# First pass of an induced-attention and two-FFN kernel: a smaller first group, two groups' x in both layouts from memory, the inducing points from another queue

## The chip, the cores and the metric

One NeuronCore of a Trainium2 chip runs the whole kernel. The metric is device time in microseconds (us) of one execution; lower is better. Engines are named as the profile names them: PE (TensorE matmul), PEld (TensorE weight load), DVE (VectorE), ACT (ScalarE), POOL (GpSimd), SP (SyncE, which here only issues DMAs; a small q behind an engine's name is its instruction queue).

## What is computed

With x of 12480 tokens x 128 and 32 inducing points of 128, all f32:

```python
def mab(q, kv):
    s = scale * (q @ kv.T); a = softmax(s)
    return a @ kv
h = mab(I, x)            # the first pass: 32 queries over all tokens
y = mab(x, h)            # every token over 32 keys
g = y @ w_in;  y = (g * clip(g + 3, 0, 6) / 6) @ w_out       # d_ff 2048
g = y @ w_in2; out = relu(g) ** 2 @ w_out2
```

Nothing after the first pass can begin before h is whole, since its softmax runs over all tokens. The four weight matrices are stored as 64-bit words that the kernel itself turns into f32, in pieces of 512 words a partition: a0 to a3 (w_in), b0 to b3 (w_out), c and d (the second FFN).

## The kernel before, in words

The span has two parts. The **first pass** (about 37 us) computes h; the rest (about 920 us) is a software pipeline over 25 chunks of up to 512 tokens. The change touches the first pass alone.

The first pass runs over eight groups g0 to g7 (`GROUPS`; each entry is a block of rows, and a block holds 4 x 128 tokens, or 4 x 48): g0 has 1024 tokens, g1 to g4 2048 each, g5 1216 (it is kept in the tile `xlast` for later), g6 and g7 1024 each. `xT` and `x` are the same tokens in two layouts in memory. For one group:

- `load_group` brings x transposed (tile `xg`, three buffers, L298; the group g5 goes to `xlast`), and makes the tile `xn` (three buffers, made in the order of the groups) for x in its natural layout.
- `scores`: 8 matmuls (L340, tile `s1`), then DVE takes the maximum (L344, into `kept`).
- x in its natural layout: `turn_x` transposes each block on PE (4 transposes, L360) and ACT copies it out (L365). For the groups in `NATURAL` (g7 alone) nothing is turned; `load_natural` reads it from memory instead (L303).
- `exps` on ACT (L350), `turn_e`: transposes of the exponentials on PE (L373) and a DVE copy (L375, L378); `accumulate`: 8 matmuls a block (L385) and an ACT copy (L389).

The order is software-pipelined by hand and kept: each engine does its instructions in the order in which the code has them. In iteration g: loads of x up to g+3, `scores(g)`, `turn_e(g-1)`, `turn_x(g)`, `exps(g)`, a tick, `accumulate(g-1)`, a tick. Ticks are numbered from 0, two an iteration, and `EARLY` says what of the weights is converted at each: tick 10 does a2's third and a3's second stage, tick 11 (the last thing of g5's iteration) a3's third stage and b0's first, tick 12 b0's second, tick 13 its third, tick 16 (after the loop's last accumulation) b1's first. A piece's first stage is an ACT multiplication of the raw words (L180) and two DVE instructions on them (L188, L192), so ACT and DVE both wait there for the piece's load; the second stage is two more on DVE (L201, L209), the third an addition on POOL (L221).

All loads are issued by SP in one fixed order, `LOADS`; `load_until` only says when the code issues them. A load whose buffer is still in use waits on SP, and everything behind it in the list waits too. At the end of the pass h is scaled and written (L447 to L464); the short chain up to the first matmuls of the pipeline (`fill` are matmuls into nothing, L261) follows.

```python
    for g in range(NG):
        load_until(("x", min(g + 3, NG - 1)))
        load_until(("n", g))
        scores(g)
        if g:
            turn_e(g - 1)
```

Of the kernel before, what the change touches and what calls it, by code (L numbers as in the profile page):

```python
# [26 lines left out]
LINE = 256  # L27


GROUPS = [(128,) * 2] + [(128,) * 4] * 4 + [(128, 128, 48), (128,) * 2, (128,) * 2]  # L30
KEPT = 5
TURN_V = {}
NATURAL = {7}


LOADS = [("x", 0), ("x", 1), ("x", 2), ("a", 0), ("x", 3), ("a", 1), ("x", 4), ("a", 2), ("a", 3),
         ("x", 5), ("b", 0), ("x", 6), ("x", 7), ("b", 1), ("n", 7), ("b", 2), ("b", 3)]

# [31 lines left out]
def induced_attention_then_two_ffn(  # L72
# [11 lines left out]
    nc = tc.nc  # L84
# [9 lines left out]
    SCALE = 1.0 / math.sqrt(D)  # L94
    NG = len(GROUPS)
    run = [sum(blocks) for blocks in GROUPS]
    assert sum(run) * J == NT and D == P and J == 4
# [185 lines left out]
    with ExitStack() as pro:  # L283
# [5 lines left out]

        row = pp.tile([P, J, M], F32, name="row")  # L290
        sel, ind, inds = (row[:, i, :] for i in range(3))
        nc.sync.dma_start(ind, indT)
        xn = {}

        def load_group(g):
            n = run[g] * J
            xg[g] = xlast if g == KEPT else pp.tile([P, n], F32, tag="xg", name="xg", bufs=3)
            nc.sync.dma_start(xg[g], xT[:, t0[g]:t0[g] + n])  # L298
            xn[g] = pp.tile([P, len(GROUPS[g]) * J, D], F32, tag="xn", name="xn", bufs=3)

# [54 lines left out]
        def turn_x(g, b):  # L355
            blk, o = GROUPS[g][b], sum(GROUPS[g][:b])
            t = pps.tile([blk, J, D], F32, tag="xt", name="xt", bufs=4)
            for j in range(J):
                i = j * run[g] + o
                nc.tensor.transpose(t[:, j, :], xg[g][:, i:i + blk], ident)  # L360
            dst = xn[g][:blk].rearrange("p (j b) d -> p b j d", j=J)[:, b]
            if b in TURN_V:
                nc.vector.tensor_copy(dst, t)
            else:
                nc.scalar.copy(dst, t)  # L365

        def turn_e(g):
            nb = len(GROUPS[g])
            t = pps.tile([P, nb, P], F32, tag="xt", name="ett", bufs=4)
            et[g] = pp.tile([P, nb, P], F32, tag="et", name="et", bufs=2)  # L370
            for b, blk in enumerate(GROUPS[g]):
                o = sum(GROUPS[g][:b])
                nc.tensor.transpose(t[:blk, b, :], es[g][:, o:o + blk], ident)  # L373
            whole_blocks = sum(blk == P for blk in GROUPS[g])
            nc.vector.tensor_copy(et[g][:, :whole_blocks], t[:, :whole_blocks])  # L375
            for b in range(whole_blocks, nb):
                blk = GROUPS[g][b]
                nc.vector.tensor_copy(et[g][:blk, b], t[:blk, b])  # L378
# [42 lines left out]
        for g in range(NG):  # L421
# [8 lines left out]
            for b in range(len(GROUPS[g])):  # L430
                if g not in NATURAL:
                    turn_x(g, b)
# [453 lines left out]
```

## Time and profile before

| | |
|---|---|
| median of 3 runs | 958.47 us (958.36 to 959.15) |
| the profiled execution: its time / its span | 959.55 us / 957.8 us |
| mean granted TensorE clock | 0.998 |
| busy share: PE, PEld, DVE, ACT, POOL | 99%, 80%, 83%, 85%, 26% |
| moved by DMA | 34.28 MB, of it 14.88 MB in the first 60 us |

Rows of a timeline read: start in us, duration in us, engine, line, operation, output<-input, how many were merged, and in brackets how long the engine had been idle and what ended that. Start times count from the span's start. A matmul's row overlaps the next one's, since matmuls are pipelined. "Landing" of a load is the time from its issue to its completion.

### The profile page before, as it was taken

Reading aid. Unit: us, or ns where it says so; the run is one execution under the profiler, and the core shown is the slowest. Engines: PE = TensorE matmul, PEld = TensorE weight load, DVE = VectorE, ACT = ScalarE, POOL = GpSimd, SP = SyncE. Lnnn points to the kernel's source line nnn. Section 1 sums busy time; section 2 is a strip of 40 time slices with the busy share of each in tenths; the row PEclk is TensorE's granted clock in tenths of the full one; section 3 lists DMA queues with packets and bytes.
Section 4 is the critical chain, followed back from the end, with each engine's and each line's share of the span. In section 5 each row is a group of like instructions: output and inputs, shape, how many; then the busy total and the mean of one; then the engine's idle time right before and its main releaser. Section 6 shows DMA issues by size and latency. Waiting matters only on the chain.

```text
span 957.8 us, 12885 instructions
## 1 busy us (share of the span) xinstructions
PE 947.5 (99%) x4609; PEld 767.7 (80%) x4609; DVE 795.1 (83%) x971; ACT 813.0 (85%) x927; POOL 248.4 (26%) x412
## 2 busy tenths in 40 slices
PE   9799999999999999999999999999999999999998
PEld 7546678888888888888888888888888888888898
DVE  5887788888888888888888888888888888888774
ACT  6668888888888888888888888888888888889887
POOL 1233222222222222222222222222222222222222
PEclk9999999999999999999999999999999999999999
DMA  9621000000100000100000100010000100000000
GB/s 363 233 69 55 5 19 23 1 22 26 42 23 12 11 23 11 56 23 9 15 23 8 48 23 7 17 55 4 19 23 3 46 23 2 22 20 2 17 12 16
DMA packets 30671, 34.28 MB, mean 36 GB/s; under 512 B 7440, under 2 KB 24080, under 8 KB 30096
## 3 DMA queue, kind: packets, MB, share of 16 engines
q1 hardware_dynamic: 30608, 33.47, 10.5%
q8 instruction: 36, 0.59, 0.3%
q14 instruction: 27, 0.22, 0.1%
HBM read 21.18 MB, written 6.39 MB: 29 GB/s over the span
## 4 chain that ended last, share of the span: by engine, by line
PE 97%; DVE 2%; issue 0%; ACT 0%; POOL 0%; DVEq 0%; POOLq 0%
PE h L726 28%; PE oacc L697 27%; PE yacc L697 25%; PE h L649 9%; PE yacc L685 3%; PE oacc L685 1%; PE xt L360 1%; PE ps L513 1%; PE s L340 1%; PE hacc L385 0%; PE fill L261 0%; DVE cve L192 0%; DVE et L375 0%; DVE cve L188 0%; DVE m L495 0%
## 5 line engine op out<-in xcount | busy, mean ns | idle before, releaser
L658 DVE SCALAR_TENSOR_TENSOR g<-g,h 128x1024 f32<-128x1024 f32 (+2 forms) x200 | 238.8, 1194 | 119.5 <-ACT g L657 116.8
L657 ACT ACTIVATE g<-h,small 128x1024 f32<-128x1024 f32 (+2 forms) x200 | 219.1, 1096 | 115.5 <-PE h L649 111.6
L761 DVE TENSOR_TENSOR lo<-g,hi 128x1024 fp32r<-128x1024 f32 (+3 forms) x193 | 228.9, 1187 | 7.8 <-PE oacc L697 4.1
L677 DVE TENSOR_TENSOR lo<-g,hi 128x1024 fp32r<-128x1024 f32 (+2 forms) x184 | 219.1, 1191 | 0.8 <-POOL hi L669 0.8
L741 ACT ACTIVATE g<-g 128x1024 f32<-128x1024 f32 (+3 forms) x201 | 206.0, 1025 | 0.2
L737 ACT ACTIVATE g<-h 128x1024 f32<-128x1024 f32 (+3 forms) x201 | 199.3, 992 | 3.3 <-PE h L726 2.1
L753 ACT CAST hi<-g 128x1024 fp32r<-128x1024 f32 (+1 forms) x186 | 191.6, 1031 | 0.0
L669 POOL TENSOR_SCALAR hi<-g 128x1024 fp32r<-128x1024 f32 (+2 forms) x182 | 187.2, 1029 | 0.0
L726 PE MATMUL h<-yh,wl 128*128 128x512 f32 (+2 forms) x400 | 153.7, 384 | 0.0
L726 PE MATMUL h<-yh,wh 128*128 128x512 f32 (+2 forms) x400 | 153.7, 384 | 0.0
L726 PE MATMUL h<-yl,wh 128*128 128x512 f32 (+2 forms) x400 | 153.7, 384 | 0.0
L649 PE MATMUL h<-at,m 128*128 128x512 f32 (+2 forms) x400 | 129.3, 405 | 2.3 <-DVE m L495 2.0
L697 PE MATMUL oacc<-hi,wh 128*128 128x512 f32 (+2 forms) x384 | 116.5, 384 | 0.0
L697 PE MATMUL oacc<-hi,wl 128*128 128x512 f32 (+2 forms) x384 | 116.4, 384 | 0.0
L697 PE MATMUL oacc<-lo,wh 128*128 128x512 f32 (+2 forms) x384 | 116.4, 384 | 0.0
L796 POOL COPY small<-lo 128x1 f32<-128x1 f32 x115 | 21.8, 189 | 344.8 <-DVE lo L677 344.8
L697 PE MATMUL yacc<-hi,wl 128*128 128x512 f32 (+2 forms) x368 | 111.2, 383 | 0.0
L697 PE MATMUL yacc<-hi,wh 128*128 128x512 f32 (+2 forms) x368 | 111.2, 383 | 0.0
L697 PE MATMUL yacc<-lo,wh 128*128 128x512 f32 (+2 forms) x368 | 111.2, 383 | 0.0
L649 PEld LDWEIGHTS h<-at,m 128*128 128x128 f32 x400 | 74.4, 188 | 26.5 <-issue 8.7
L726 PEld LDWEIGHTS h<-yl,wh 128*128 128x128 f32 x400 | 75.1, 188 | 14.6
L726 PEld LDWEIGHTS h<-yh,wh 128*128 128x128 f32 x400 | 75.1, 188 | 14.2
(121 smaller groups left out, 920.5 us busy)
## 6 DMA issues: line engine op xcount, KB each, us to landing
outT<-osb SPq DMA_DIRECT2D x23, 256.0 KB, 2.2
xc<-in_xT SPq DMA_DIRECT2D x9, 512.0 KB, 4.6
xg<-in_xT SPq DMA_DIRECT2D x4, 1024.0 KB, 7.1
at<-ah SPq DMA_DIRECT2D x168, 16.0 KB, 1.8
at<-al SPq DMA_DIRECT2D x168, 16.0 KB, 1.8
raw<-in_w1a SPq DMA_DIRECT2D x4, 512.0 KB, 8.8
raw<-in_w1b SPq DMA_DIRECT2D x4, 512.0 KB, 7.5
raw<-in_w2a SPq DMA_DIRECT2D x4, 512.0 KB, 8.3
```

What stands on the lines that cost most here:

```text
L649: nc.tensor.matmul(h1[k][:, u, :size[c]], lhsT=m4[:, f * P:(f + 1) * P], rhs=a_t[c], start=True, stop=True)
L657: nc.scalar.activation(g1[k], h, AF.Relu, bias=three)
L658: nc.vector.scalar_tensor_tensor(out=g1[k], in0=g1[k], scalar=6.0, in1=h, op0=ALU.min, op1=ALU.mult)
L669: nc.gpsimd.tensor_scalar(out=hi1[k], in0=g1[k], scalar1=1.0, scalar2=1.0, op0=ALU.mult, op1=ALU.mult)
L677: nc.vector.tensor_tensor(out=lo1[k], in0=g1.pop(k), in1=hi1[k], op=ALU.subtract)
L685: nc.tensor.matmul(acc, lhsT=w[:, f * P:(f + 1) * P], rhs=g[:, u, :], start=(p == 0 and u == 0), stop=(p == NP - 1 and u == 1),)
L697: nc.tensor.matmul(acc, lhsT=w[:, f * P:(f + 1) * P], rhs=g[:, u, :], start=(p == 0 and n == 0), stop=(p == NP - 1 and n == 5),)
L726: nc.tensor.matmul(h2[k][:, u, :size[c]], lhsT=w, rhs=y, start=(n == 0), stop=(n == 2))
L737: nc.scalar.activation(g2[k][:, u, :], h[:, u, :n], AF.Relu)
L741: nc.scalar.activation(g2[k][:, u, :], g2[k][:, u, :], AF.Square)
L753: nc.scalar.copy(hi2[k][:, u, :], g2[k][:, u, :])
L761: nc.vector.tensor_tensor(out=lo2[k][:, u, :], in0=g[:, u, :], in1=hi2[k][:, u, :], op=ALU.subtract)
```

## The change

The first group has one block (512 tokens) instead of two; g6 has three blocks (1536 tokens) instead of two. So all groups together still hold 12480 tokens. g6 is added to the groups whose natural x is read from memory, so its `turn_x` goes and a load `("n", 6)` of 768 KB comes. The list of loads has that load between those of x for g6 and g7, and b0's load moves from ahead of g6's x to behind g7's. The load of the inducing points is issued by ACT instead of SP. `EARLY` is not changed.

```diff
-GROUPS = [(128,) * 2] + [(128,) * 4] * 4 + [(128, 128, 48), (128,) * 2, (128,) * 2]
+GROUPS = [(128,)] + [(128,) * 4] * 4 + [(128, 128, 48), (128,) * 3, (128,) * 2]
-NATURAL = {7}
+NATURAL = {6, 7}
 LOADS = [("x", 0), ("x", 1), ("x", 2), ("a", 0), ("x", 3), ("a", 1), ("x", 4), ("a", 2), ("a", 3),
-         ("x", 5), ("b", 0), ("x", 6), ("x", 7), ("b", 1), ("n", 7), ("b", 2), ("b", 3)]
+         ("x", 5), ("x", 6), ("n", 6), ("x", 7), ("b", 0), ("n", 7), ("b", 1), ("b", 2), ("b", 3)]
...
-        nc.sync.dma_start(ind, indT)
+        nc.scalar.dma_start(ind, indT)
```

## Rows read from the trace of the kernel before

**Rows 1.** Busy time of the page: us (share), instructions of each engine.
```profile
PE 947.5 (99%) x4609; PEld 767.7 (80%) x4609; DVE 795.1 (83%) x971; ACT 813.0 (85%) x927; POOL 248.4 (26%) x412
```
**Rows 2.** Timeline of PE and PEld in the first pass.
```profile
1.36 4.10 PE L261 MATMUL fill<-ident 128*128 128x128 f32 x18 [1.36 <-POOL ident masks.py:199]
5.39 1.08 PE L340 MATMUL s<-xg,row 128*32 128x256 f32 x8
6.41 1.14 PE L360 MATMUL xt<-ident,xg 128*128 128x128 f32 x8
...
7.47 0.16 PEld L340 LDWEIGHTS s<-xg,row 128*32 128x32 f32 x8 [0.17 <-DMA xg<-in_xT]
...
22.75 1.08 PE L385 MATMUL hacc<-xn,et 128*32 128x128 f32 x32
...
27.07 0.61 PE L340 MATMUL s<-xg,row 128*32 128x256 f32 x8
...
29.75 1.00 PE L385 MATMUL hacc<-xn,et 128*32 128x128 f32 x24 [0.71 <-DVE et L375]
```
**Rows 3.** Busy time by stretch: each engine's us (instructions), granted clock, DMA share, GB/s.
```profile
20.00:25.00 5.00, 5.00 (x75) 3.92 (x68) 4.30 (x9) 4.25 (x12) 1.29 (x2) 1.00 1.04 403
26.00:27.00 1.00, 1.00 (x35) 0.83 (x36) 0.97 (x2) 1.00 (x5) 0.26 (x1) 1.00 0.28 96
```
**Rows 4.** Timeline of SP's queue: when loads are issued.
```profile
0.74 0.39 SPq L292 DMA_DIRECT2D row<-in_indT  x1
...
1.18 0.42 SPq L298 DMA_DIRECT2D xg<-in_xT  x1
...
12.70 0.47 SPq L152 DMA_DIRECT2D raw<-in_w1b  x1
...
19.03 0.43 SPq L152 DMA_DIRECT2D raw<-in_w1b  x1
...
27.35 0.38 SPq L303 DMA_DIRECT2D xn<-in_x  x1
...
28.42 0.50 SPq L152 DMA_DIRECT2D raw<-in_w1b  x1
```
**Rows 5.** DMA issues, those five loads in that order: KB, us to landing.
```profile
xg<-in_xT SPq DMA_DIRECT2D x1, 512.0 KB, 3.7
...
raw<-in_w1b SPq DMA_DIRECT2D x1, 512.0 KB, 11.4
...
raw<-in_w1b SPq DMA_DIRECT2D x1, 512.0 KB, 8.9
...
xn<-in_x SPq DMA_DIRECT2D x1, 512.0 KB, 3.9
...
raw<-in_w1b SPq DMA_DIRECT2D x1, 512.0 KB, 6.1
```
**Rows 6.** Waits of SP's queue, 0 to 62 us: us in total, times, longest.
```profile
SPq L303 <- PE hacc L385: 7.8, 1, 7.8
```
**Rows 7.** DVE timeline around tick 11, and L192's durations (ns, min/median/max).
```profile
27.18 0.42 DVE L188 TENSOR_SCALAR cve<-raw 128x512 uint32<-128x512 uint32 x1
...
29.29 0.41 DVE L375 COPY et<-ett 128x256 f32<-128x256 f32 x1
...
L192 DVE TENSOR_SCALAR cve<-cve x7: 426/428/1393, 13.8 to 42.7; 128x512 f32<-128x512 f32 x7
```
**Rows 8.** Timeline of POOL at that time.
```profile
27.41 1.33 POOL L221 TENSOR_TENSOR wa<-cve,cva 128x512 int32<-128x512 int32 x1 [1.16 <-DVE cve L209]
```
**Rows 9.** PE after an idle stretch in the pipeline's first microseconds, timeline.
```profile
46.33 0.73 PE L649 MATMUL h<-at,m 128*128 128x512 f32 x2 [1.96 <-DVE m L495]
...
48.01 3.32 PE L685 MATMUL yacc<-g,w 128*128 128x512 f32 x4
...
52.19 1.88 PE L685 MATMUL yacc<-g,w 128*128 128x512 f32 x4
```
**Rows 10.** The same stretch by half microseconds: PE busy, granted clock, DMA share, GB/s.
```profile
47.50:48.00 0.50, 0.50 (x1) 0.50 0.68 240
```

## The prediction

> **What bounds the kernel now.** The busy times come first: PE is busy for 99% of the span [rows 1], so the pipeline after the first pass has no room, and whatever moves the end of the pass moves the end of the kernel by as much. The change touches the pass alone, so the rest is read there. PE's timeline shows it at work from 1.36 us, first on 18 matmuls into nothing and then on one group after another [rows 2]. It is the pace-maker up to the scores of g6 at 27.07; then it stands for 0.71 us, and `accumulate(5)` at 29.75 is let go by DVE's copy L375. So the last part of the pass hangs on DVE, and DVE's order around tick 11 says why: b0's first stage (L188 at 27.18, then L192) stands ahead of the maximum of g6 and of that copy [rows 7]. The third view is the stretches: the DMA engines are at a share of 1.04 with 403 GB/s from 20 to 25 us, and idle soon after, 0.28 at 26 to 27 us [rows 3]. A load is thus late or early by the bytes ahead of it.
>
> **The start.** Moving the inducing points off SP lets the first x be issued at 0.74 instead of 1.18 us, 0.44 earlier [rows 4]; ACT has nothing to do so early. That x was issued at 1.18 and landed 3.7 later, at 4.9 [rows 4, 5], while the fill matmuls still ran to about 5.4 [rows 2], so the first scores start no earlier than 0.3 us before, whatever the load does. What the smaller group gives lies in the PE work: scores and turning of g0 took 5.39 to 6.41 and 6.41 to 7.47, each halves, so 1.04 us goes. The scores of g1 waited 0.17 us for their x at 7.47 [rows 2]; that load now comes 0.44 + 0.64 us sooner (0.64 for 256 KB less ahead of it, worked out below), which just covers it. `accumulate(0)` and `turn_e(0)` lose a block too: 1.08/4 = 0.27 us [rows 2] and a little. I take 1.35 us for all of it, between 0.3 (only the start moves) and 1.6. The loads behind move 1.08, so up to 0.27 of the 1.35 may be waited away again.
>
> **g6's turning removed.** 12 transposes and their copies on ACT go. They are costed at nothing: PE stood idle for 0.71 us right behind them, waiting for DVE [rows 2]. DVE is not relieved. The block that left g0 is now in g6, at the end of the pass where nothing hides it: 0.27 us of `accumulate(6)` and up to 0.2 us (half of the 0.41 us that two blocks' copy takes [rows 7]) of each of DVE's copy and maximum. Between 0.3 and 0.7; I take 0.5 us lost.
>
> **The load of b0, the term that decides.** b0 was issued at 12.70 and landed 11.4 later, at 24.1; DVE wanted it at 27.18, so 3.1 us were spare. b1 was issued at 19.03 and landed 8.9 later, at 27.9. Between the two landings the queue brought 3 x 512 KB in 3.83 us, 1.28 us for 512 KB [rows 4, 5, 7]. After the change b0 stands behind g6's x (768 KB), g6's natural x (768 KB) and g7's x (512 KB), less 256 KB of g0: 1792 KB more, 4.48 us, and 0.44 earlier from the start: 28.1 us at best. But tick 11 is not moved, and the pass runs 1.35 us ahead, so ACT and DVE stop for b0 at about 25.8. The maximum of g6, the copy for `accumulate(5)` and everything of g6 and g7 stand behind it.
>
> It gets later if g6's natural x waits. SP's queue shows how its fellow did: g7's natural x waited 7.8 us on `accumulate` [rows 6] and went out at 27.35 [rows 4], just after `accumulate(4)`, though g2's buffer had long been free: buffers go round in the order in which the tiles are made, and g7's is g4's. By that g6's is g3's, free after `accumulate(3)`, which ended at about 23.65 (22.75 and its length [rows 2]), so now 22.3. g7's x and b0 queue on SP behind that wait. From the issue, g7's natural x took 3.9 us to 31.25, and b3, issued at 28.42, landed 6.1 later at 34.5, 1024 KB behind it [rows 4, 5]. So g6's lands at 22.3 + 3.9 + 0.64 = 26.8, and b0, also 1024 KB behind, between 26.8 + 2.56 = 29.4 and 26.8 + 3.27 = 30.1. I take 29.8, nearer to the late row, since that is the one which had a natural x at the head of the queue.
>
> From L188's start to `accumulate(5)` it was 29.75 - 27.18 = 2.57 us. In this L192 took 1.39 where its median is 0.43 [rows 7], beside POOL's addition at 27.41 [rows 8]; that addition (a3's third stage) will be over before b0 lands. 2.57 - 0.97 = 1.60 us is left. So `accumulate(5)` starts at 29.8 + 1.60 = 31.4, 1.65 us later than before (1.25 to 1.95). All that the start won is gone: DVE's clock for the rest is the landing of b0.
>
> **PE's clock.** PE has no turning to do meanwhile. With the pass 1.35 ahead, scores and `turn_e` end at about 27, and it stands until 31.4, over 4 us. Later in the trace it stood for 1.96 us before 46.33; from 47.5 on the granted clock is 0.50, that is 1.2 GHz, and four matmuls took 3.32 us where the next four took 1.88 [rows 9, 10]. The gap of 0.71 us is followed by no such thing. So 0 to 2.9 us (twice that loss) may be added; I take 1.7, that row's 1.44 and a little for the short matmuls behind, since the new gap is longer than the one that lost the clock.
>
> **Sum.** 1.65 + 0.5 + 1.7 = 3.85 us, of which the start's gain is already part. The profiled execution took 959.55 us (span 957.8); with 3.85 it is 963.4. It lies 1.1 above the median of the runs, 958.47, to which I add the same: 962.3 us. This case by itself reaches from 958.5 + 1.25 + 0.5 = 960.2 to 958.5 + 1.95 + 0.5 + 2.9 = 963.8.
>
> **Rivals.** *g6's natural x does not wait.* If the buffers are handed out by who is ready, g0's or g1's is free when SP comes to it, and b0 lands at 28.1. Then `accumulate(5)` starts at 29.7 as before, 0.5 is lost for the block and 0 to 1.7 for the clock (PE stands 2.7 us): 959.0 to 960.6 us. For it: nothing in the code forbids it. Against it: the 7.8 us that g7's waited.
>
> *b0 is in time, not slower.* The decision is at b0's landing: at 27.65 or before, 1.60 later `accumulate(5)` is 0.5 us sooner than before, which pays for the block; at 25.8 or before DVE doesn't wait at all, and the gain is 1.35 - 0.5 = 0.85, 957.6 us. It takes a b0 that overtakes the 1280 KB of natural x and g7's x ahead of it. The landings of before come in the order of issue, b0 24.1 and b1 27.9 with two loads between, which speaks against it. The Trainium skill, in DMA: Bandwidth & Descriptors, "Queues, rings and completion order", says that completion is not in order per issuing engine, as data transfers carry no barrier between them. By that rule b0 could land ahead of what was issued before it and this case would hold; no row here shows a load doing so.
>
> A further chance on this side: if the stretch at 1.2 GHz from 47.5 us does not come back in the shifted timing, 1.44 us are won in any case [rows 9].
>
> **How the numbers follow.** A difference of 0.2%, 1.9 us (956.55 to 960.4), is about what a measurement of this kernel can tell from none. The forecast gets 0.58, the first rival 0.20, the second 0.17; 0.05 is left for what I don't see. Slower by over 0.2%: 0.52 of the forecast, 0.04 of the first rival, 0.02 of the rest, 0.58. Faster by over 0.2% needs the second rival with the clock's 1.44 us as well: 0.08 with part of the rest. The same: 0.34. The range of 8 in 10 goes from 957.0, a little under the second rival's own time, to 964.5, a little beyond the forecast's upper end for a clock that stays low longer; the forecast's own range is 960.2 to 963.8.
>
> **What the profile would show.** Right: b0's load issued at about 23 and landing at 29 to 30; ACT's L180 and DVE's L188 idle for some 4 us before tick 11, ended by a DMA on `raw`; `accumulate(5)` at 31 to 32; PE idle from 27, with matmuls of twice the length behind it. The scores of g1 at 6.1 to 6.5 and of g2 over a microsecond earlier than before. The first rival: g6's natural x issued at about 14, right behind g6's x. The second: b0's L188 at 26 with no wait. The prediction is wrong if DVE does not wait for b0, or if the pass's end, the write of h, comes less than 1 us later than before.

## The result, and the profile after

The changed kernel takes 966.16 us (median of 8 executions, 961.31 to 966.53) against 958.93 us for the kernel before (8 on the same chip, 958.36 to 959.9): a ratio of 1.0061, 95% interval 1.0046 to 1.0077. It is slower, as forecast, but by 7.2 us, where 3.85 had been summed up and 964.5 was the upper end of the range. The profiled execution took 966.22 us with a span of 964.4, which is 6.6 above the span profiled before.

PE's timeline in the changed kernel answers to [rows 2] and, in its last row, to [rows 9]:

```profile
5.40 0.62 PE L340 MATMUL s<-xg,row 128*32 128x128 f32 x8
5.94 0.66 PE L360 MATMUL xt<-ident,xg 128*128 128x128 f32 x4
6.53 1.07 PE L340 MATMUL s<-xg,row 128*32 128x512 f32 x8
...
25.91 0.83 PE L340 MATMUL s<-xg,row 128*32 128x384 f32 x8
26.67 0.55 PE L373 MATMUL ett<-ident,es 128*128 128x128 f32 x3
30.34 1.66 PE L385 MATMUL hacc<-xn,et 128*32 128x128 f32 x24 [3.12 <-DVE et L375]
...
41.67 1.92 PE L540 MATMUL ps<-ht,xlast 128*128 128x32 f32 x8
...
52.92 0.73 PE L649 MATMUL h<-at,m 128*128 128x512 f32 x2 [1.86 <-DVE m L495]
```

Read down the start times. The scores of g6 come 1.16 us earlier than before (25.91 against 27.07). Then PE stands for 3.12 us, and `accumulate(5)` starts 0.59 later than before (30.34 against 29.75). So far little is lost. But the same `accumulate(5)`, with 24 matmuls of the same shape, now lasts 1.66 us instead of 1.00, and the first matmuls of the pipeline (L540) start at 41.67. Before they started at 36.91:

```profile
36.91 1.05 PE L540 MATMUL ps<-ht,xlast 128*128 128x32 f32 x8 [0.21 <-DVE ht L464]
```

From `accumulate(5)` to L540 it was 7.16 us and is 11.33; from L540 to the third pair of up-projections (L649; before at 46.33) it was 9.42 and is 11.25. So 0.59 + 4.17 + 1.83 = 6.59 us, the whole difference of the spans, and nearly all of it lies behind the wait. There PE's stops are about as long as before (0.65 and 0.30 us for the copies of g6 and g7, where it was 0.52 and 0.40), but the groups of matmuls take up to nearly twice as long.

DVE, then SP's queue, then the DMA issues of the three loads in that order (answers to [rows 7, 4, 5]) show what held `accumulate(5)`:

```profile
28.59 0.43 DVE L188 TENSOR_SCALAR cve<-raw 128x512 uint32<-128x512 uint32 x1 [2.46 <-DMA raw<-in_w1b]
```

```profile
14.37 0.38 SPq L303 DMA_DIRECT2D xn<-in_x  x1
17.49 3.69 SPq L298 DMA_DIRECT2D xg<-in_xT  x1
21.23 0.43 SPq L152 DMA_DIRECT2D raw<-in_w1b  x1
```

```profile
xn<-in_x SPq DMA_DIRECT2D x1, 768.0 KB, 11.5
...
xg<-in_xT SPq DMA_DIRECT2D x1, 512.0 KB, 9.7
...
raw<-in_w1b SPq DMA_DIRECT2D x1, 512.0 KB, 7.3
```

DVE stood 2.46 us for b0, which landed at 21.23 + 7.3 = 28.5, behind the natural x of g6 (25.9) and the x of g7 (27.2): in the order of issue, 1.3 us for each 512 KB. But the natural x of g6 went out at 14.37, not at 22.

The stretches by microsecond (columns as in [rows 3]: after the five engines the granted clock, the DMA share and GB/s) show the third thing:

```profile
28.00:29.00 1.00, 0.00 (x0) 0.00 (x0) 0.41 (x1) 0.42 (x1) 0.00 (x0) 1.00 0.98 269
29.00:30.00 1.00, 0.00 (x0) 0.00 (x0) 0.97 (x4) 0.25 (x1) 0.00 (x0) 0.87 1.13 365
30.00:31.00 1.00, 0.66 (x16) 0.59 (x16) 0.96 (x4) 0.67 (x2) 0.00 (x0) 0.50 1.07 378
34.00:35.00 1.00, 0.51 (x12) 0.48 (x16) 0.73 (x3) 0.16 (x2) 0.00 (x0) 0.50 1.04 424
...
39.00:40.00 1.00, 1.00 (x8) 1.00 (x5) 0.57 (x3) 1.00 (x4) 0.00 (x0) 0.50 0.09 33
...
45.00:46.00 1.00, 1.00 (x5) 0.75 (x4) 0.86 (x4) 0.45 (x1) 0.00 (x0) 0.50 0.00 0
46.00:47.00 1.00, 1.00 (x8) 1.00 (x7) 0.96 (x3) 0.33 (x2) 0.00 (x0) 0.60 0.00 0
47.00:48.00 1.00, 1.00 (x12) 1.00 (x11) 0.97 (x3) 0.00 (x0) 0.00 (x0) 1.00 0.00 0
```

In PE's idle stretch, at about 29.7, the clock goes from 1.00 to 0.50 (from 2.4 to 1.2 GHz), and it comes back only near 46.8: some 17 us, the whole rest of the first pass and the head of the pipeline. The stretch of [rows 10] lasted 3.4 us, from 47.5 to about 50.9 (kernel before, by half microseconds, columns as in [rows 10]):

```profile
50.50:51.00 0.50, 0.50 (x2) 0.59 0.11 37
```

The slower clock also turns a cover into a delay. The matmuls into nothing that stand behind the end of the pass took 0.74 and 1.91 us before, and PE stood idle for 0.21 and 0.36 us after them. Now they take 1.31 and 2.68 us, PE does not stop behind them, and the chain that ended last runs through them (start, us):

```profile
40.49 1.13 PE fill L261 x5
...
45.45 2.47 PE fill L261 x16
```

From where DVE's results for L540 and L611 were ready (about 40.8 and 46.5, with the 0.15 us that passed in the trace before) to where these start (41.67 and 47.68) it is 0.7 and 1.0 us. As an estimate, 1.7 us of the loss are thus these fills; no run takes them out.

### The profile page after: what moved, and what is told of

It is laid out like the page before. It is cut to its first block, busy times and chain, and to the rows that moved or that the text cites. A ratio compares the mean times of both kernels' runs of the same rounds, so it can differ in the third digit from the quotient of the medians.

```text
span 964.4 us, 12856 instructions
## 1 busy us (share of the span) xinstructions
PE 952.5 (99%) x4597; PEld 771.1 (80%) x4597; DVE 794.9 (82%) x971; ACT 812.6 (84%) x924; POOL 248.8 (26%) x412
## 4 chain that ended last, share of the span: by engine, by line
PE 97%; DVE 1%; DMA 1%; ACT 0%; issue 0%; POOL 0%; SPq 0%; POOLq 0%; DVEq 0%
PE h L726 28%; PE oacc L697 26%; PE yacc L697 25%; PE h L649 9%; PE yacc L685 3%; PE oacc L685 1%; PE fill L261 1%; DMA raw<-in_w1b 1%; PE xt L360 1%; PE hacc L385 1%; PE ps L513 1%; PE s L340 1%; PE ett L373 0%; PE mixed L485 0%; ACT g L657 0%
## 5 line engine op out<-in xcount | busy, mean ns | idle before, releaser
L649 PE MATMUL h<-at,m 128*128 128x512 f32 (+2 forms) x400 | 129.3, 405 | 2.2 <-DVE m L495 1.9
L649 PEld LDWEIGHTS h<-at,m 128*128 128x128 f32 x400 | 74.4, 188 | 26.4 <-issue 8.7
```

Of the source, the lines that this page charges most:

```text
L649: nc.tensor.matmul(h1[k][:, u, :size[c]], lhsT=m4[:, f * P:(f + 1) * P], rhs=a_t[c], start=True, stop=True)
```

## The experiments

The executions of one kernel fall into groups by their mean granted clock over the span, so this table counts them (number of executions, mean us):

```
                                       1.000, 0.999   0.998         0.996, 0.993   0.991, 0.989
before, the three sessions below       41, 958.50     49, 959.76    2, 963.36
after (8)                                                           1, 961.31      7, 966.06
1 b0 early (12)                         4, 957.88      1, 959.29    3, 959.73      4, 963.73
2 b0 a tick later (12)                  2, 957.72      6, 958.87    3, 962.54      1, 964.49
3 fills (11)                            8, 959.61      3, 961.20
4 g6 turned on PE (11)                  4, 957.79      7, 959.18
5 inducing points alone (12)            5, 958.26      7, 959.65
6 b0 early, fills (12)                 12, 957.89
7 g6 turned on PE, fill (12)           12, 958.10
8 before, fill (12)                    11, 958.46                   1, 963.23
9 b0 early, a tick later, fills (11)   11, 957.49
10 before, fill, a tick later (11)     11, 957.86
```

The kernel before itself is of two kinds, 1.26 us apart; its median is the one or the other as the larger share falls. Ratios below are to it, over all of its executions of the same session.

**1. b0's load back in front**, nothing else moved:

```diff
-         ("x", 5), ("x", 6), ("n", 6), ("x", 7), ("b", 0), ("n", 7), ("b", 1), ("b", 2), ("b", 3)]
+         ("x", 5), ("b", 0), ("x", 6), ("n", 6), ("x", 7), ("n", 7), ("b", 1), ("b", 2), ("b", 3)]
```

> The changed kernel with b0's load back ahead of g6's x, nothing else moved. Theory (the wait for b0 leaves PE idle for 3.1 us, PE drops to 1.2 GHz, and the low clock costs most of the 7 us): b0 lands at about 23, DVE's L188 runs at about 26 without a wait, accumulate(5) starts near 28.7, the granted clock stays at 1.00 up to 45 us, and the time is 957.5 to 959, 0.7 below the kernel before. Rival (the bytes added, 768 KB of natural x, hold up the loads of the pass in any place): the wait moves to another load, x or natural x of g6 or g7, and the time stays above 962.

Measured: 959.70 us (957.3 to 963.95), ratio 1.0012 (0.9997 to 1.0028): by the medians 6.5 us of the 7.2 are back, but the time is not below the kernel before, as the theory had it. In its trace, an execution of 963.45 us, DVE no longer waits for b0 and `accumulate(5)` starts at 28.82, as the theory said:

```profile
28.82 1.00 PE L385 MATMUL hacc<-xn,et 128*32 128x128 f32 x24 [1.51 <-DVE et L375]
...
39.26 1.92 PE L540 MATMUL ps<-ht,xlast 128*128 128x32 f32 x8
```

But the clock did not hold, against the theory. PE's idle stretch is now 1.51 us, and at 30 us the clock still fell, to come back at 43.7:

```profile
30.00:31.00 1.00, 1.00 (x10) 0.47 (x3) 0.38 (x2) 0.15 (x1) 0.83 (x1) 0.53 1.08 382
...
43.00:44.00 1.00, 1.00 (x8) 1.00 (x7) 0.93 (x4) 0.78 (x2) 0.00 (x0) 0.65 0.00 0
```

L540 is reached 10.44 us after `accumulate(5)` though no load is late. The table has 4 of the 12 executions like that and 4 with a clock of 1.000 at 957.88, 5.9 us apart from the same code. The load's lateness is thus one way to make PE stand still; this run points to the clock afterwards as what costs the microseconds, and kernel 3 tests it.

**2. b0's stages one tick later**, the changed kernel's loads kept:

```diff
-    10: "a2.3 a3.2", 11: "a3.3 b0.1", 12: "b0.2", 13: "b0.3", 16: "b1.1",
+    10: "a2.3 a3.2", 11: "a3.3", 12: "b0.1", 13: "b0.2", 14: "b0.3", 16: "b1.1",
```

> The changed kernel with its own order of loads; only b0's stages are moved one tick later (12, 13, 14 in place of 11, 12, 13). Theory (what hurts is only that the maximum of g6 and the copy for accumulate(5) stand behind b0 on DVE): accumulate(5) starts at about 27.6 and PE's longest idle stretch falls under 2 us; DVE still waits for b0 until 28.5, now ahead of the maximum of g7; the clock stays high and the time is 957 to 959. Rival (b0 late is enough, wherever it is consumed): the stall only moves behind accumulate(5), the clock falls all the same, and the time is 963 to 966.

Measured: 959.10 us (957.68 to 964.49), ratio 1.0008 (0.9994 to 1.0022). `accumulate(5)` starts at 27.84, and the wait for b0 moves behind it and shrinks; now `accumulate(6)` has the idle stretch before it:

```profile
27.84 1.00 PE L385 MATMUL hacc<-xn,et 128*32 128x128 f32 x24 [0.53 <-DVE et L375]
...
31.89 1.01 PE L385 MATMUL hacc<-xn,et 128*32 128x128 f32 x24 [2.01 <-DVE et L375]
```

Its profiled execution was one of the 0.998 kind, and the clock fell in it too, behind the 2.01 us, at 32.5, but was back at 35.9 (columns as above):

```profile
32.00:33.00 1.00, 1.00 (x25) 0.65 (x25) 0.48 (x1) 0.09 (x2) 0.46 (x1) 0.74 1.09 381
33.00:34.00 1.00, 0.75 (x4) 0.66 (x4) 0.44 (x2) 0.22 (x1) 0.00 (x0) 0.50 1.11 397
...
35.00:36.00 1.00, 1.00 (x19) 0.58 (x15) 0.93 (x4) 0.69 (x2) 0.00 (x0) 0.56 1.04 426
```

So a low stretch in the end of the pass need not last 17 us. The rival is half right: 4 of the 12 executions have mean clocks of 0.993 or 0.991 and take 962.4 to 964.5. None of these was profiled, so how long their clock stayed low is not shown. A stall in another place, 2 us long, costs the 4 to 6 us in some executions only.

**3. Matmuls into nothing while DVE waits.** Nothing of the wait is changed:

```diff
+            if g == NG - 2:
+                fill(24, pps, "xt", 4)
```

> The changed kernel with 24 matmuls into nothing (about 2.9 us at 2.4 GHz) between turn_e(5) and accumulate(5), so that PE works while DVE waits for b0 as before. The wait stays: accumulate(5) still starts at 30.3. Theory (the clock costs most of it): the granted clock stays at 1.00 from 27 to 45 us, h is written at about 37.4 instead of 40.5, and the time is 959 to 960.5. Rival (the wait itself and the larger g6 at the pass's end cost it, the clock being a bystander): the time stays at 964 to 966.5.

Measured: 959.76 us (959.15 to 961.57), ratio 1.0008 (1.0000 to 1.0017). This is the run that tells the two theories apart, because b0 is as late as in the changed kernel (DVE's wait for it is 2.82 us here) and `accumulate(5)` starts at 30.14 instead of 30.34:

```profile
26.50 2.78 PE L261 MATMUL fill<-ident 128*128 128x128 f32 x24
30.14 1.00 PE L385 MATMUL hacc<-xn,et 128*32 128x128 f32 x24 [0.85 <-DVE et L375]
31.07 0.64 PE L340 MATMUL s<-xg,row 128*32 128x256 f32 x8
...
37.76 1.05 PE L542 MATMUL ps<-ht,xlast 128*128 128x32 f32 x8 [0.19 <-DVE ht L466]
```

```profile
30.00:31.00 1.00, 0.86 (x24) 0.53 (x24) 0.96 (x4) 0.52 (x2) 0.00 (x0) 1.00 1.10 386
```

The clock stays at 1.00, each matmul has its old length, and the same code from `accumulate(5)` to the pipeline's first matmuls (two lines lower in this file) takes 7.62 us instead of 11.33; from there to the third pair of up-projections it is 9.42 (47.18), as before, instead of 11.25. Useless work on an idle engine wins back 6.4 us of the 7.2. What is left at a full clock, 959.61 against 958.50, is 1.1 us; 0.85 of it stands at the pipeline's first matmuls in the trace (37.76 against 36.91) and is the late b0 and the larger g6.

**4. g6 turned on PE**, no natural load for it:

```diff
-NATURAL = {6, 7}
+NATURAL = {7}
...
-         ("x", 5), ("x", 6), ("n", 6), ("x", 7), ("b", 0), ("n", 7), ("b", 1), ("b", 2), ("b", 3)]
+         ("x", 5), ("x", 6), ("x", 7), ("b", 0), ("n", 7), ("b", 1), ("b", 2), ("b", 3)]
```

> The changed kernel without the natural load of g6: g6's x is turned on PE as before (12 transposes, 1.4 us), so 768 KB less stand ahead of b0. Theory: b0 lands near 26.6, DVE's wait for it falls to about half a microsecond, PE has the transposes in the gap, accumulate(5) starts near 28.9, the clock holds, time 957.5 to 959. Rival (b0's place behind g7's x is what hurts, with or without the natural load): a wait of more than 2 us stays, the clock falls, 962 or more.

Measured: 959.06 us (957.41 to 959.47), ratio 0.9994 (0.9986 to 1.0003). DVE does not wait for b0 (L188 at 26.27), `accumulate(5)` starts at 28.98 after 0.21 us of idle PE:

```profile
28.98 1.00 PE L385 MATMUL hacc<-xn,et 128*32 128x128 f32 x24 [0.21 <-DVE et L375]
```

None of the 11 executions has a clock below 0.998; the median is 0.06 above the 959 that was expected. The run changes two things, since without the 768 KB b0 comes in time as well. But in kernel 1 DVE doesn't wait for b0 either, and there PE stands for 1.51 us where it is 0.21 here: the difference is the turning. The work that the change took off PE, costed at nothing in the prediction, was what kept PE busy there. By kinds of execution this kernel is 0.6 to 0.7 us under the kernel before, with the small first group and the earlier start gained and the block in g6 paid.

**5. The inducing points from ACT's queue alone**, in the kernel before:

```diff
-        nc.sync.dma_start(ind, indT)
+        nc.scalar.dma_start(ind, indT)
```

> The kernel before with the one line changed that has ACT issue the inducing points' load. Theory (the first scores are held by the fill matmuls, and the loads have slack afterwards): x of g0 is issued at 0.74 and lands 0.4 earlier, the scores of g1 start up to 0.4 earlier than 7.47, later nothing is gained but that; time 958.5 to 959.5, within 0.5 of the kernel before. Rival (the whole start of the changed kernel comes from this line): the scores of g1 start 0.9 earlier.

Measured: 959.25 us (958.01 to 960.42), ratio 0.9996 (0.9986 to 1.0005), no difference that the kinds would not explain; at a full clock 958.26 against 958.50. The scores of g1 start at 7.25 instead of 7.47, 0.2 earlier, and the first scores, at 5.39, not at all.

**6 to 8. Fills where PE stands.** Kernel 6 is kernel 1 with 11 fills before `accumulate(5)`; all three have 14 before the pipeline's third pair of up-projections, where PE stood for 1.96 us [rows 9]. Kernel 7 is kernel 4 with that, kernel 8 the kernel before with that alone:

```diff
+        if k == 2:
+            fill(14, ap_, "y", 1)
         on(up1, k)
```

> The changed kernel with b0's load back in front and with 11 matmuls into nothing before accumulate(5) and 14 before the pipeline's third pair of up-projections (about 1.3 and 1.7 us of otherwise idle PE). Theory (PE's idle stretches decide the clock, and the clock alone makes one execution of a kernel 2 to 6 us longer than the next): every execution has a mean clock of 0.998 or more, none lies above 959.5, the median is 957.2 to 958, faster than the kernel before. Rival (the executions differ for another reason, in the loads): the spread of 957.3 to 964 stays.

Measured: 957.96 us (957.26 to 958.53), ratio 0.9984 (0.9975 to 0.9992). No load and no group differs from kernel 1; its 957.3 to 963.95 has become 957.3 to 958.5.

> The kernel with the small first group, the larger g6 turned on PE and no natural load for it, with 14 matmuls into nothing before the pipeline's third pair of up-projections. Theory: the stretch at 1.2 GHz at 47 to 51 us goes, all executions are at a mean clock of 1.00 with 957.3 to 958.2, median about 957.6. Rival: the fills come too late for the clock or delay that pair, and the median stays at 959.

Measured: 957.90 us (957.66 to 959.27), ratio 0.9986 (0.9977 to 0.9994). All 12 have a clock of 0.999 or 1.000, but the median is above the 957.6 expected and three lie above 958.2 (958.69, 958.75, 959.27). The clock is not the reason there; what is stays open.

> The kernel before with the same 14 matmuls into nothing at that place and nothing else. Theory (its executions are of two kinds, at 958.4 with a clock of 1.000 and at 959.7 with 0.998, by whether the clock falls behind PE's idle stretch at 44 to 46 us): only the first kind is left, median 958.4 to 958.6. Rival (the two kinds come from elsewhere): both kinds stay.

Measured: 958.45 us (958.26 to 963.23), ratio 0.9993 (0.9982 to 1.0004). In the trace the third pair waits 0.43 us instead of 1.96, and the four matmuls behind it take 1.88, not 3.32 [rows 9]:

```profile
46.38 0.73 PE L649 MATMUL h<-at,m 128*128 128x512 f32 x2 [0.43 <-DVE m L495]
...
47.81 1.88 PE L685 MATMUL yacc<-g,w 128*128 128x512 f32 x4
```

The kind at 0.998 is gone. One execution in 12 was at 963.23 with a clock of 0.993, as were 2 of the 92 of the kernel before; none of these was profiled, and where their clock fell stays open.

**9 and 10. DVE's order.** Kernel 9 is kernel 6 with b0's stages a tick later as in 2 and 4 fills instead of 11 before `accumulate(5)`; kernel 10 is kernel 8 with the same tick.

> The kernel with b0's load back in front and fills (14 before the pipeline's third pair, 4 instead of 11 before accumulate(5)), with b0's three stages one tick later. Theory (what paces the end of the pass is DVE's order: b0's first stage ahead of the maximum of g6 and the copy for accumulate(5)): accumulate(5) follows the scores of g6 by 1.8 us instead of 2.8, the clock stays at 1.00, median 956.5 to 957.4, below every other kernel here. Rival (b0's stages only move to a place where they hold up g7 as much): the median stays at 957.9 to 958.2.

Measured: 957.49 us (957.09 to 957.91), ratio 0.9983 (0.9974 to 0.9992), all executions at a clock of 1.000. `accumulate(5)` follows the scores of g6 by 1.84 us where it was 2.82 in kernel 6 (29.46 behind 26.64) and 2.68 before:

```profile
26.40 0.83 PE L340 MATMUL s<-xg,row 128*32 128x384 f32 x8
...
27.55 0.60 PE L261 MATMUL fill<-ident 128*128 128x128 f32 x4
28.24 1.00 PE L385 MATMUL hacc<-xn,et 128*32 128x128 f32 x24
29.64 0.64 PE L340 MATMUL s<-xg,row 128*32 128x256 f32 x8 [0.41 <-DMA xg<-in_xT]
```

The last row shows what is late next: the x of g7, by 0.41 us. The median is not quite as low as hoped, 957.5 instead of 957.4 at most.

> The kernel before, its groups and loads untouched, with the 14 fills before the pipeline's third pair and b0's three stages one tick later. Theory as for the other: accumulate(5) starts at about 29.1 instead of 29.75 (PE's transposes of g6 end there), 957.6 to 958, and the rest of the other's lead is the small first group and the natural load of g6. Rival: no change against the kernel with the fills alone, 958.4.

Measured: 957.73 us (957.56 to 958.63), ratio 0.9987 (0.9978 to 0.9996). `accumulate(5)` starts at 28.96, with PE no longer idle before it. With everything that holds the clock and frees DVE put into the kernel before, its own groups and loads are only 0.4 us behind kernel 9 at a full clock (957.86 against 957.49). Kernel 9 beats both kernels of the comparison.

## Why the prediction was wrong in its size

The step that failed is the price of PE's low clock, put at 1.7 us and at most 2.9; it was 5.5. A second step, the reason for b0's lateness, was wrong as well and made the wait too long by 1.1 us.

**The start** was right. The first scores did not move (5.40, against 5.39) although their x landed at 0.74 + 2.9 = 3.6, because the fill matmuls stood before them; g1's came at 6.53, 0.94 earlier, just past the 6.1 to 6.5 given; with the block of `accumulate(0)` the pass ran 1.16 ahead at g6. I had taken 1.35. That agreement is in part luck: in the eight traces with this start the scores of g1 begin at 6.09 to 7.02, so the gain there is 0.45 to 1.4 us from one execution to the next.

**The block in g6** was right: from `accumulate(5)` to L540 it is 7.62 us at a full clock (kernel 3) where it was 7.16, 0.46, and 0.5 was summed.

**The load of b0** was right in its mechanism, and the step before it wrong. The prediction read from the 7.8 us wait of g7's natural x [rows 6] that buffers go round in the order in which the tiles are made, and sent g6's to wait for g3's buffer until 22.3. It went out at 14.37, just after `accumulate(1)` ended at 14.27, so by its time it got g1's buffer, which no longer held anything needed; in all six traces that have this load it goes out so. That was the first rival's case, with b0 at 28.1, and its sign in the profile; b0 landed at 28.5. So `accumulate(5)` came 0.59 late, not 1.65. The 1.60 us from L188 to it were 1.75. The rival had been given 0.20, and its price of 959.0 to 960.6 missed too, by the clock.

The reading of the 7.8 us was wrong in that g2's buffer was not free: g5's tile is written before g7's and needs it. Counted by the first write in the code, g7's load comes after g4, g5 and g6 have the three buffers, and g4's is the first to come free. The load for g6 stands in iteration 4 ahead of `turn_x(4)`, the first write of g4's tile; there g1, g2 and g3 have the buffers, and g1's comes free first. That count fits every such load in the traces; no run was made to test it.

**The clock** is the term that was mis-sized, and it overturns the sum: 1.7 us were summed and 2.9 allowed, from a low stretch of 3.4 us; it lasted 17 us and cost 4.17 + 1.83 - 0.46 = 5.5 us in the profiled execution, which is also what lies between it and kernel 3 on the same two stretches, 11.33 - 7.62 and 11.25 - 9.42. I had taken the price of a low stretch from one place and carried it to another. In [rows 9, 10] the clock fell and PE then had back-to-back matmuls (busy 0.50 of each 0.50 us) and was soon at 2.4 GHz again. After 30 us the end of the pass gives PE short groups with waits on DVE between them, busy 0.51 to 1.00 of a microsecond up to 38 us. At half the clock each PE link of that serial chain is longer, and each is on the path, the fills among them. Why the clock stayed low so long is open. The waits of the end of the pass alone don't explain it: from 38 to 46.8 PE was busy for 0.94 to 1.00 of each microsecond and the clock was still at 0.50, while in kernel 2 it came back in the same end of the pass after 3.4 us. With 0.59 and 0.46 as the other terms came out, 5.5 for the clock gives the 6.6 measured.

**The second rival** did not occur: b0 landed after everything issued ahead of it. The Trainium skill says in DMA: Bandwidth & Descriptors, "Queues, rings and completion order", that completion need not be in order for one issuing engine; the changed kernel's trace doesn't show it, the landings being 25.9, 27.2 and 28.5 in the order of issue. The extra chance named with it, that the low stretch at 47 us might not come back, did not come true either: behind 52.92 the clock fell once more (L685's four matmuls take 2.88 us there).

## What to carry to other kernels

An idle engine can be a cover: before work is taken off PE as free because PE waits right behind it, look at what the clock does if that wait grows by the work's length. Price a fall of the clock by the work that comes after it in that place, and not by a fall elsewhere (here 1.44 us in one place and 5.5 in another), and give it a wide range, since the mean clock differed between executions of one code. Where a kernel's executions differ by more than their noise, sort them by mean granted clock before comparing medians; a few matmuls into nothing in the gap (here 2.8 us of them for 6.4 us) are a quick test of whether the clock is the reason, and sometimes the repair.

## What was not expected of the hardware

- In kernel 1 one idle stretch of PE of 1.5 us was followed by a low clock in the execution that was profiled; 4 of its 12 executions lost some 6 us like that one, and 4 others lost nothing. Of the changed kernel, where it is 3.1 us, all 8 executions have a mean clock of 0.996 or less, 7 of them 0.991 or less.
- The inducing points' 16 KB took 3.1 us to land from ACT's queue (0.73 to 3.8), 1.8 from SP's when they were the first load. The fill matmuls covered it.
- SP needs mostly 0.3 to 0.6 us to issue a load, but in the changed kernel the issue of g7's x lasted 3.69 us (17.49 to 21.18) with some 3 MB of loads under way, and 3.65 to 5.31 in the other kernels that load g6's natural x. For b0 it did no harm, since it landed 1.3 us behind g7's x, at the queue's pace. What held it was not tried.
